# Strassen's seven products in the last matrix product of a retention and bilinear feed-forward kernel

## The chip, the core and the metric

The kernel runs on one NeuronCore of a Trainium2 chip. The core has a matrix engine (TensorE, PE in the profile; its weight loads are listed apart as PEld), a vector engine (VectorE, DVE), a scalar engine (ScalarE, ACT), a general engine (GpSimd, POOL) and an engine that here only issues DMAs (SyncE, SP). Each has its own instruction queue and works through it in order; semaphores tie the queues together. TensorE reads SBUF and writes PSUM; VectorE and ScalarE carry results from PSUM to SBUF. The metric is the device time of one execution in microseconds, lower is better.

## The reference

```python
q, k, v = float32 [8, 8, 576, 64]                  # batch, head, position, head dim
scores = (q @ k.transpose(0, 1, 3, 2)) / sqrt(64)
gamma  = 1.0 - 2.0 ** (-5.0 - arange(8))           # one decay per head
D[h, i, j] = gamma[h] ** (i - j) if i >= j else 0
ret = (scores * D) @ v
x   = ret.transpose(0, 2, 1, 3).reshape(4608, 512) # tokens x (head, dim)
a, b = x @ w_a, x @ w_b                            # both [512, 1536]
out = ((a * b) @ w_out).astype(float32)            # w_out [1536, 512]
```

The first part is retention: attention with an exponential decay in place of a softmax. The second is a bilinear feed-forward layer over all 4608 tokens. The last product, with w_out, is the one that is changed.

## The kernel before

**Feed-forward blocks.** The 4608 tokens go through the feed-forward part in ten blocks: 512, 256, 256 and then seven of 512 tokens (`blocks`, L111). The seven start at token 1024. `ffn_block` (L850) is a generator that writes one block's instructions. For each of the twelve slices F of 128 of the 1536 inner columns it makes four products with w_a into a PSUM tile `pa` (L872), which ScalarE copies to `ha` in bf16 (L880), four products with w_b into `pb` (L887), and VectorE multiplies the two into the bf16 tile `hT` (L892), which holds the inner activations of the block as [128 inner rows, 12 slices, 512 tokens]. Then come the rows: for each 128 tokens, twelve products with `hT` as the stationary operand and w_out (`wo_sb`) as the moving one, 512 columns wide, into a tile `po` (L908). ScalarE and VectorE copy `po` to `osb` in turn (L917, L919), and SP stores it. The final 128 tokens are done in pieces of 256, 128 and 128 columns, each in a `po` tile of its own.

All of `pa`, `pb` and `po`, and the tiles `kv` below, come from one ring of four PSUM tiles of 512 float32 columns, one PSUM bank each (`ps_ffn`, tag "ab", L89). A product into a new tile waits until the last reader of the tile four places earlier has ended. `hT` has one buffer, `osb` eight.

**Retention.** The tokens are also cut into eighteen groups of 256, a "pair" of 128 each (`PAIRS`, L50). For group n, `load_pair` (L140) has SP load q, k and v into a ring of staging tiles (`stage`, four buffers each of qf, kf, vf). `ahead(n)` (L509) has POOL cast q and k to bf16 (L519, L523) and multiply v by its decays (L530). `turn(n)` (L536) has SP transpose q and k by DMA (L542) and, from n = 11 on, load group n+2. `stretch(into, outof)` (L756) writes the products: for the group `outof` the part of the output that comes from states (`open_outputs`, `from_states`, L670), for `into` the sums of keys by values (`keyed`, L573, into two tiles `kv` of the ring of four) and the scores (`matched`, L642, which needs the transposed q and k), and for `outof` the part from its own keys (`keys_into`, L683). The work of other engines that follows is put on a list `later`: four additions that read `kv` (VectorE, L600), two calls of `scaled` (VectorE writes the group's x, L696), a conversion with the first mask, a conversion with the second mask (ScalarE L603 to L611, VectorE L651). Every `pop()` in the feed-forward code writes the next item of that list into the queues; `flush()`, at each block's end and each stretch's start, writes all that are left. The last stretches and `outputs_alone` (L746) write their sums of two PSUM tiles in a constant tile `both` first (`summing`, L730).

**Order.** The program is written by hand order (`manual_schedule`). The main loop at the end walks through all blocks; each `yield` of `ffn_block` gives the cost of what was just written, in units of one 512-column product, and whether this is an edge. At an edge every entry of `todo` whose due time has come is called. A block of 512 tokens counts 96 units for w_a and w_b and 48 for the rows. In the rows there is an edge after every four products. Most `stretch` calls are due 116 and 44 units before the start of a block (`starts`), the casts 70 and the transposes 38 units before their stretch (L1084 to L1108); those of the early groups have fixed times, for example `stretch(8, 7)` at unit 408.

**Stores.** From the fourth block on `store` is called right after a copy. Rows of the first blocks wait in `held` and are stored at listed times, since SP and the DMA engines are then busy with loads.

## Time and profile before

| what | value |
|---|---|
| median of 3 runs | 324.75 us (324.59 to 324.81) |
| profiled execution: span, first to last instruction | 323.1 us |
| median less span (what lies around the profiled span) | 1.65 us |
| granted TensorE clock, mean | 0.999 of full speed |
| TensorE busy | 313.8 us, 97% |
| VectorE busy | 166.2 us, 51% |
| ScalarE busy | 130.7 us, 40% |
| POOL busy | 118.8 us, 37% |
| 512-column products of the rows (L908) | 379 ns each as recorded |
| weight loads | 98 ns each, beside the products |

The profile has one execution. A matmul's recorded duration holds its way through the pipeline, so two in a row overlap; the rate of TensorE is read from their starts. A line of the timeline gives start, duration, engine, line, operation, written tile <- read tiles, shapes and count, and in brackets how long the engine was idle before and what ended that. A line of groups gives count, busy us, mean ns of one, idle before and its releasers. A line of a window gives its length, then the busy us of PE, PEld, DVE, ACT and POOL, the granted clock, the busy share of the DMA engines and GB/s.

### The profile page before, as it was taken

To read this page: it belongs to the slowest core of one execution; us is meant where nothing else is said; L and a number is where in the kernel's file an instruction comes from. 1 tells how busy PE (TensorE), PEld (TensorE's weight loads), DVE (VectorE), ACT (ScalarE), POOL (GpSimd) and SP (SyncE) were. 2 spreads that over 40 slices of the span, in tenths; PEclk is the share of its full clock that TensorE was granted. 3 is DMA by queue.
4 is the path that set the end of the run, shared out by engine and by line. 5 is a ranking of instruction groups with operands and counts; after the bars stand their busy time and mean duration, and the time that the engine had idled before them with its cause. 6 is when DMAs were issued, how large, how long until landed. Compare 5 with 4: busy or idle time off the path is not lost.

```text
span 323.1 us, 8622 instructions
## 1 busy us (share of the span) xinstructions
PE 313.8 (97%) x3569; PEld 164.0 (51%) x3607; DVE 166.2 (51%) x296; ACT 130.7 (40%) x289; POOL 118.8 (37%) x159
## 2 busy tenths in 40 slices
PE   7899999999999999999999999999999999999996
PEld 3554457778444555454454545454545444444444
DVE  5745346667437654745374527561666256514311
ACT  7745653436435533523253324342433243313321
POOL 4990077564744355447264305450520000000000
PEclk9999999999999999999999999999999999999999
DMA  8999999999899989999999168935940510031013
GB/s 215 253 201 206 260 228 180 192 181 206 180 189 227 199 199 204 287 208 232 230 220 215 70 143 191 212 79 145 210 72 26 137 37 2 2 97 32 1 25 107
DMA packets 146487, 50.90 MB, mean 158 GB/s; under 512 B 126736, under 2 KB 141968, under 8 KB 146448
## 3 DMA queue, kind: packets, MB, share of 16 engines
q1 hardware_dynamic: 140112, 45.37, 66.3%
q0 software_dynamic: 5808, 4.72, 9.3%
q8 instruction: 28, 0.46, 0.6%
q10 hardware_dynamic: 528, 0.26, 0.3%
q14 instruction: 11, 0.09, 0.1%
HBM read 37.75 MB, written 9.44 MB: 146 GB/s over the span
## 4 chain that ended last, share of the span: by engine, by line
PE 93%; DMA 2%; POOL 1%; issue 1%; SPq 1%; DVE 0%; POOLq 0%
PE pb L887 29%; PE pa L872 28%; PE po L908 27%; DMA vf<-in_v_dram 2%; PE po L834 2%; PE o L683 1%; PE sc L642 1%; PE o L670 1%; PE kv L573 1%; SPq L159 1%; POOL vb L326 1%; PE pa L823 1%; PE o L465 0%; PE tp L334 0%; POOL wb_sb L266 0%
## 5 line engine op out<-in xcount | busy, mean ns | idle before, releaser
L892 DVE TENSOR_TENSOR hT<-ha,pb 128x512 bf16<-128x512 bf16 (+1 forms) x120 | 75.8, 632 | 91.4 <-PE pb L887 83.3
L887 PE MATMUL pb<-xT,wb_sb 128*128 128x512 bf16 (+1 forms) x473 | 111.3, 357 | 0.5
L880 ACT CAST ha<-pa 128x512 bf16<-128x512 f32 (+1 forms) x120 | 64.8, 542 | 112.8 <-PE pa L872 108.3
L872 PE MATMUL pa<-xT,wa_sb 128*128 128x512 bf16 (+1 forms) x457 | 108.0, 357 | 1.1 <-issue 0.6
L908 PE MATMUL po<-wo_sb,hT 128*128 128x512 bf16 (+2 forms) x419 | 89.6, 367 | 1.6 <-issue 1.4
L887 PEld LDWEIGHTS <-wb_sb 128*128 128x128 bf16 x480 | 46.9, 98 | 46.3
L872 PEld LDWEIGHTS <-wa_sb 128*128 128x128 bf16 x472 | 45.4, 98 | 44.8 <-DVE sums L600 0.2
L908 PEld LDWEIGHTS <-hT 128*128 128x128 bf16 x432 | 40.4, 98 | 44.4
L519 POOL CAST qkb<-qf 64x1024 bf16<-64x1024 f32 x15 | 15.4, 1030 | 65.4 <-DMA qf<-in_q_dram 64.4
L530 POOL TENSOR_TENSOR vb<-vf,vs 128x1024 bf16<-128x1024 f32 (+1 forms) x17 | 28.8, 1699 | 13.0 <-DMA vf<-in_v_dram 4.9
L919 DVE COPY osb<-po 128x512 f32<-128x512 f32 (+2 forms) x16 | 10.4, 649 | 38.8 <-PE po L908 38.8
L917 ACT COPY osb<-po 128x512 f32<-128x512 f32 (+1 forms) x20 | 11.4, 572 | 46.3 <-PE po L908 43.4
L519 POOL CAST qkb<-kf 64x1024 bf16<-64x1024 f32 (+1 forms) x17 | 15.9, 933 | 16.7 <-DMA kf<-in_k_dram 16.3
L600 DVE TENSOR_TENSOR sums<-kv,sums 128x256 f32<-128x256 f32 x44 | 18.6, 423 | 2.8 <-PE kv L573 0.8
L651 DVE TENSOR_TENSOR sT<-sc,mask 128x512 bf16<-128x512 f32 x30 | 19.5, 680 | 0.0
L523 POOL CAST qkb<-kf 64x512 bf16<-64x512 f32 (+1 forms) x34 | 18.6, 574 | 1.0
L523 POOL CAST qkb<-qf 64x512 bf16<-64x512 f32 x30 | 17.6, 614 | 0.6
L696 DVE TENSOR_TENSOR xT<-o,qs 128x512 bf16<-128x512 f32 x24 | 15.4, 680 | 2.6 <-PE o L683 2.6
L603 ACT CAST states<-sums 64x512 bf16<-64x512 f32 x26 | 16.0, 617 | 0.3
L316 POOL CAST qkb<-kf 128x512 bf16<-128x512 f32 x4 | 2.5, 612 | 15.9 <-DMA kf<-in_k_dram 15.9
L360 DVE TENSOR_TENSOR sT<-sc,mask_s 128x1024 bf16<-128x1024 f32 x6 | 7.3, 1222 | 1.5 <-PE sc L352 1.3
L935 PE MATMUL w<-ones 128*128 128x512 bf16 x17 | 6.5, 497 | 1.5 <-DVE idxp_f L204 1.5
(96 smaller groups left out, 173.5 us busy)
## 6 DMA issues: line engine op xcount, KB each, us to landing
qf<-in_q_dram SPq DMA_DIRECT2D x32, 256.0 KB, 4.7
vf<-in_v_dram SPq DMA_DIRECT2D x32, 256.0 KB, 5.0
kf<-in_k_dram SPq DMA_DIRECT2D x31, 256.0 KB, 5.1
out_dram<-osb SPq DMA_DIRECT2D x25, 256.0 KB, 3.2
out_dram<-osb SPq DMA_DIRECT2D x21, 128.0 KB, 2.7
wo_sb<-in_moe_w_out_dram POOLq DMA_DIRECT2D x3, 512.0 KB, 15.9
qf<-in_q_dram SPq DMA_DIRECT2D x8, 128.0 KB, 3.6
kf<-in_k_dram SPq DMA_DIRECT2D x8, 128.0 KB, 3.6
```

What stands on the lines that cost most here:

```text
L519: nc.gpsimd.tensor_copy(qkb[0:64, w, e], t[0:64, e])
L523: nc.gpsimd.tensor_copy(to[:, :, 1 - r], fro[:, :, r])
L530: nc.gpsimd.tensor_tensor(vb[:, e].rearrange("p (h d) -> p h d", d=D), t[:, e].rearrange("p (h d) -> p h d", d=D), decay[:, at], op=ALU.mult)
L600: nc.vector.tensor_tensor(sums[:, i], own, prev, op=ALU.add)
L603: return [lambda r=r: nc.scalar.copy(to(half(1 - r)), fro(half(r))) for r in (0, 1)]
L651: nc.vector.tensor_tensor(sT[:, on].rearrange("p c k s -> p (c k) s"), sc[:, on].rearrange("p c k s -> p (c k) s"), mask3.unsqueeze(1).to_ ...
L696: nc.vector.tensor_tensor(x_of(t0, 128).rearrange("p c (a s) -> p c a s", a=2), o[:, :, :, kp].rearrange("p a c s -> p c a s"), qs[:, :, s ...
L872: nc.tensor.matmul(pa[:, 0:n], wa_sb[:, c, fs], xT[:, c], start=(c == 0), stop=(c == NC - 1))
L880: nc.scalar.copy(ha[:, 0:n], pa[:, 0:n])
L887: nc.tensor.matmul(pb[:, 0:n], wb_sb[:, c, fs], xT[:, c], start=(c == 0), stop=(c == NC - 1))
L892: nc.vector.tensor_tensor(hT[:, F, 0:n], has[F][:, 0:n], pb[:, 0:n], op=ALU.mult)
L908: nc.tensor.matmul(po[:, 0:width], hT[:, F, u * 128:(u + 1) * 128], wo_sb[:, F, cols], start=(F == 0), stop=(F == NF - 1))
```

## The change

From token 1024 on (group 4, `MIXED`) the product with w_out is done by Strassen's scheme. A group of 256 tokens is the left matrix, with even and odd tokens as its two row halves and the inner slices F even and odd as its two contraction halves; w_out's column halves of 256 are the right one's. With a11, a12, a21, a22 (row half, contraction half) and b11 to b22, seven half-size products are made, each of six matmuls of 256 columns, 42 a group in place of 24 of 512 columns.

What comes with it:

- `scaled` writes x so that even and odd tokens of a group lie apart, as two operations of 256 columns in place of one of 512.
- `weight_sums`: ten VectorE operations of 768 bf16 elements make b11+b22, b11+b12, b21+b22 and, in place, b12-b22 and b21-b11, at times 150 to 180 and 290 to 314 of the list.
- `row_sums`: per block ten VectorE operations on `hT`, all operands bf16 in SBUF, five of 1024 elements from F = 7 on (two after each F) and five of 512 after F = 11, before the edge of F = 11. Two of each five are in place.
- `rows_mixed`: the products and their combination. Products 3 and 4 go to the halves of one tile (m34), product 1 to a tile m1, products 5 and 2 to the halves of a tile m52; products 7 and 6 are later added to the halves of m34. ScalarE copies m34 and m1 to SBUF, VectorE combines.
- It offers an edge only at the end of a group, and `total` counts 21/24 for the rows, so that a changed block has 138 units.
- A group is stored by one DMA of 512 KB (four of 128 KB for the two groups made of batch ends, three pieces for the last).
- `stage` goes from four buffers to three, `osb` from eight tiles to four of double size, `both` moves into the ring of vf, and some early constants give up their space to the new tiles when the first changed block begins.

```diff
@@ pools @@
+    MIXED = 4
-    stage = pool("stage", 4)
+    stage = pool("stage", 3)
-    o_pool = pool("osb", 8)
+    o_pool = pool("osb", 4)
...
+    wo_sums = big.tile([128, 3, NF // 2, DM // 2], BF16)
@@ scaled @@
+            if n >= MIXED:
+                at = s0 + kp * step
+                x = x_of(place(n) * 256, 256).rearrange(
+                    "p c (k q a s) -> p q c a k s", k=2, q=2, a=2)[:, kp]
...
+                for a in (0, 1):
+                    nc.vector.tensor_tensor(x[:, :, a], of[:, a], by[:, :, a],
+                                            op=ALU.mult)
+                return
@@ summing @@
-    both = const.tile([128, 2, 2, HP, 64], FP32)
+        both = stage.tile([128, 2, 2, HP, 64], FP32, tag="vf", name="both")
@@ new functions @@
+    def weight_sums(step):
...
+        out, one, other, op = [(to[0], b11, b22, ALU.add),
+                               (to[1], b11, b12, ALU.add),
+                               (to[2], b21, b22, ALU.add),
+                               (b12, b12, b22, ALU.subtract),
+                               (b21, b21, b11, ALU.subtract)][step // 2]
+        nc.vector.tensor_tensor(out, one, other, op=op)
+
+    def row_sums(hT, sums, p0, p1):
+        even, odd = (hT[:, 2 * p0:2 * p1].rearrange(
+            "p (f e) (g k s) -> p e k f g s", e=2, g=2, k=2)[:, e]
+            for e in (0, 1))
+        a11, a21, a12, a22 = even[:, 0], even[:, 1], odd[:, 0], odd[:, 1]
+        to = [sums[:, i, p0:p1] for i in range(3)]
+        return [lambda e=e: nc.vector.tensor_tensor(*e[:3], op=e[3])
+                for e in ((to[0], a11, a22, ALU.add),
+                          (to[2], a12, a22, ALU.subtract),
+                          (a12, a11, a12, ALU.add),
+                          (to[1], a21, a11, ALU.subtract),
+                          (a21, a21, a22, ALU.add))]
+
+    def rows_mixed(G, hT, sums, g):
+        t0 = 256 * g
+        def product(to, way, ps, begins):
+            for p in ps:
+                even, odd = 2 * p, 2 * p + 1
+                rows, cols = {
+                    1: (sums[:, 0, p, g], wo_sums[:, 0, p]),
+                    2: (hT[:, even, t0 + 128:t0 + 256], wo_sb[:, even, 0:WIDE]),
+                    3: (hT[:, even, t0:t0 + 128], wo_sb[:, even, WIDE:]),
+                    4: (hT[:, odd, t0 + 128:t0 + 256], wo_sb[:, odd, 0:WIDE]),
+                    5: (hT[:, odd, t0:t0 + 128], wo_sb[:, odd, WIDE:]),
+                    6: (sums[:, 1, p, g], wo_sums[:, 1, p]),
+                    7: (sums[:, 2, p, g], wo_sums[:, 2, p])}[way]
+                nc.tensor.matmul(to, rows, cols, start=(begins and p == 0),
+                                 stop=True, skip_group_check=True)
+                yield 0.5, False
...
+        own, lo, hi = bank("m34")
+        for part in (range(NP2 - 1), (NP2 - 1,)):
+            yield from product(lo, 3, part, True)
+            yield from product(hi, 4, part, False)
+        straight = late["parts"].tile([128, 512], FP32, tag="m34", name="straight")
+        nc.scalar.copy(straight, own)
+        pop()
+        first, one, _ = bank("m1")
+        yield from product(one, 1, range(NP2), True)
+        ones_ = late["parts"].tile([128, WIDE], FP32, tag="m1", name="m1s")
+        nc.scalar.copy(ones_, one)
+        pop()
+        cross, five, two = bank("m52")
+        yield from product(five, 5, range(NP2), True)
+        pop()
+        yield from product(two, 2, range(NP2), False)
+        less = late["parts"].tile([128, 2, WIDE], FP32, tag="m52", name="less")
+        nc.vector.tensor_tensor(
+            less, ones_.unsqueeze(1).to_broadcast([128, 2, WIDE]),
+            cross.rearrange("p (k m) -> p k m", k=2), op=ALU.subtract)
+        flat = osb.rearrange("p k m -> p (k m)")
+        nc.vector.tensor_tensor(flat[:, WIDE:3 * WIDE], cross, straight,
+                                op=ALU.add)
...
+        pop()
+        for way, to, at, i in ((7, hi, slice(0, WIDE), 0),
+                               (6, lo, slice(3 * WIDE, 4 * WIDE), 1)):
+            yield from product(to, way, range(NP2), False)
+            nc.vector.tensor_tensor(flat[:, at], to, less[:, i], op=ALU.add)
...
+            pop()
+        if not last:
+            store_mixed(G, osb)
+        yield 0, True
@@ ffn_block, after the multiplication into hT and its pop() @@
+                if tok0 >= 256 * MIXED:
+                    if F == 7:
+                        chores += row_sums(hT, sums, 0, 4)
+                    elif F == NF - 1:
+                        chores += row_sums(hT, sums, 4, 6)
+                    for _ in range(2 if F < NF - 1 else len(chores)):
+                        if chores:
+                            chores.pop(0)()
...
+        if tok0 >= 256 * MIXED:
+            for g in range(n // 256):
+                yield from rows_mixed(tok0 // 256 + g, hT, sums, g)
+            return
@@ planner @@
-    def total(n):
-        return NF * 2 * NC * n / 512 + NF * n / 128
+    def total(n, mixed):
+        return NF * 2 * NC * n / 512 + (21 / 24 if mixed else 1) * NF * n / 128
...
+    todo += [(150 + 6 * step, weight_sums, (step,)) for step in range(6)]
+    todo += [(290 + 8 * step, weight_sums, (6 + step,)) for step in range(4)]
```

More of the change, by code (lines that the diff above doesn't have):

```diff
@@ L86, with pools_mixed @@
     ha_pool = pool("ha", 6)
-    o_pool = pool("osb", 8)
+    o_pool = pool("osb", 4)
+    late, early = {}, ExitStack()
+    begin = early.enter_context(tc.tile_pool(name="begin", bufs=1))
+    ctx.push(early)
+    def pools_mixed():
+        if not late:
+            early.close()
+            for name in ("hsum", "parts"):
+                late[name] = early.enter_context(
+                    tc.tile_pool(name=name, bufs=1))
     PS = bass.MemoryType.PSUM
@@ L180 @@
     make_identity(nc, identity)
-    mask_s = const.tile([128, 2, 2, 64], BF16)
+    mask_s = begin.tile([128, 2, 2, 64], BF16)
     nc.gpsimd.memset(mask_s, 1.0)
@@ L199, in make_masks @@
                 pattern=[[1, 64]], channel_multiplier=-1)
-    ones = const.tile([128, 512], BF16)
+    ones = begin.tile([128, 512], BF16)
     nc.vector.memset(ones, 1.0)
@@ L214 @@
                              bias=0.0, scale=-math.log(gammas[h]))
-    qs_o = const.tile([128, HP, 256], FP32)
+    qs_o = begin.tile([128, HP, 256], FP32)
     qs = const.tile([128, HP, S + 64], FP32)
@@ L250, in pair_tables @@
             make_qs(qs, (step - 5) // 2, s0, s0 + part)
-    state_after = const.tile([128, 2, HP, 128], BF16)
+    state_after = begin.tile([128, 2, HP, 128], BF16)
     own_sums = [const.tile([128, HP, 64], FP32, name=f"own{n}")
@@ L694, in scaled @@
         def scaled(kp):
+            if n >= MIXED:
+                at = s0 + kp * step
+                x = x_of(place(n) * 256, 256).rearrange(
+                    "p c (k q a s) -> p q c a k s", k=2, q=2, a=2)[:, kp]
+                by = qs[:, :, at:at + 128].rearrange(
+                    "p c (a s k) -> p c a k s", a=2, k=2)
+                of = o[:, :, :, kp].rearrange(
+                    "p a c (s k) -> p a c k s", k=2)
+                for a in (0, 1):
+                    nc.vector.tensor_tensor(x[:, :, a], of[:, a], by[:, :, a],
+                                            op=ALU.mult)
+                return
             t0 = place(n) * 256 + kp * 128
@@ L841, in rows_together @@
                     continue
-                osb = o_pool.tile([128, DM], FP32, tag="osb", name="osb")
+                osb = half_of(o_pool, u, [DM], FP32, "osb")
                 if u % 2 == 0:
@@ L848, in rows_together @@
                 yield 1, True
+    WIDE = DM // 2
+    def weight_sums(step):
+        p0 = 3 * (step % 2)
+        even, odd = (wo_sb[:, 2 * p0:2 * p0 + 6].rearrange(
+            "p (f e) m -> p e f m", e=2)[:, e] for e in (0, 1))
+        b11, b12 = even[:, :, 0:WIDE], even[:, :, WIDE:]
+        b21, b22 = odd[:, :, 0:WIDE], odd[:, :, WIDE:]
+        to = [wo_sums[:, i, p0:p0 + 3] for i in range(3)]
+        out, one, other, op = [(to[0], b11, b22, ALU.add),
[4 more added lines that the diff above has]
+        nc.vector.tensor_tensor(out, one, other, op=op)
@@ new lines, in store_mixed @@
+    def store_mixed(G, osb, cols=slice(0, 2 * DM)):
+        n = place(G)
+        for kp, r0, m, b, s0 in rows_of(n):
+            if n in LEFT:
+                p0 = kp * 64 + r0 // 2
+                m //= 2
+            elif kp == 1:
+                continue
+            else:
+                p0, m = 0, 128
+            rows = out[b * S + s0:b * S + s0 + 2 * m].rearrange(
+                "(p two) c -> p (two c)", two=2)
+            nc.sync.dma_start(rows[:, cols],
+                              osb[p0:p0 + m].rearrange("p k c -> p (k c)")
+                              [:, cols])
@@ new lines, in rows_mixed, with bank @@
+    def rows_mixed(G, hT, sums, g):
[14 more added lines that the diff above has]
+                yield 0.5, False
+        def bank(name):
+            t = ps_ffn.tile([128, 512], FP32, tag="ab", name=name)
+            return t, t[:, 0:WIDE], t[:, WIDE:]
+        NP2 = NF // 2
+        last = G == NP - 1
+        osb = o_pool.tile([128, 2, DM], FP32, tag="osb", name="osb2")
+        own, lo, hi = bank("m34")
[21 more added lines that the diff above has]
+                                op=ALU.add)
+        if last:
+            store_mixed(G, osb, slice(WIDE, 3 * WIDE))
+        pop()
[3 more added lines that the diff above has]
+            nc.vector.tensor_tensor(flat[:, at], to, less[:, i], op=ALU.add)
+            if last:
+                store_mixed(G, osb, at)
+            pop()
+        if not last:
+            store_mixed(G, osb)
+        yield 0, True
@@ L853, in ffn_block @@
         hT = h_pool.tile([128, NF, 512], BF16, tag="h", name="hT")
+        chores = []
+        if tok0 >= 256 * MIXED:
+            pools_mixed()
+            sums = late["hsum"].tile([128, 3, NF // 2, 2, 128], BF16, tag="hsum",
+                                  name="hsum")
         f0 = 0
@@ L898, in ffn_block @@
             yield from rows_together(tok0, hT, (0, 1))
+        if tok0 >= 256 * MIXED:
+            for g in range(n // 256):
+                yield from rows_mixed(tok0 // 256 + g, hT, sums, g)
+            return
         for u in range(2 if tb == 0 else 0, n // 128):
-            final = tok0 + (u + 1) * 128 == NTOK
-            osb = o_pool.tile([128, DM], FP32, tag="osb", name="osb")
-            edges = (0, DM // 2, 3 * DM // 4, DM) if final else (0, DM)
-            for part in range(len(edges) - 1):
-                cols = slice(edges[part], edges[part + 1])
-                po = ps_ffn.tile([128, 512], FP32, tag="ab", name="po")
-                width = cols.stop - cols.start
-                for F in range(NF):
-                    nc.tensor.matmul(po[:, 0:width],
-                                     hT[:, F, u * 128:(u + 1) * 128],
-                                     wo_sb[:, F, cols],
-                                     start=(F == 0), stop=(F == NF - 1))
-                    if F in (2, 5, 8):
-                        pop()
-                    if F < NF - 1:
-                        yield width / 512, F % 4 == 3
-                if n == 256 or (u + part) % 2 == 0:
-                    nc.scalar.copy(osb[:, cols], po[:, 0:width])
-                else:
-                    nc.vector.tensor_copy(osb[:, cols], po[:, 0:width])
-                if tb < 3:
-                    held.append((tok0 // 128 + u, cols, osb))
-                else:
-                    store(tok0 // 128 + u, cols, osb)
-                pop()
-                yield width / 512, True
+            osb = half_of(o_pool, u, [DM], FP32, "osb")
+            po = ps_ffn.tile([128, 512], FP32, tag="ab", name="po")
+            for F in range(NF):
+                nc.tensor.matmul(po, hT[:, F, u * 128:(u + 1) * 128],
+                                 wo_sb[:, F],
+                                 start=(F == 0), stop=(F == NF - 1))
+                if F in (2, 5, 8):
+                    pop()
+                if F < NF - 1:
+                    yield 1, F % 4 == 3
+            if n == 256 or u % 2 == 0:
+                nc.scalar.copy(osb, po)
+            else:
+                nc.vector.tensor_copy(osb, po)
+            held.append((tok0 // 128 + u, slice(0, DM), osb))
+            pop()
+            yield 1, True
     gate = const.tile([1, 64], BF16)
@@ L1029 @@
             starts[i] = at
+        at += total(n, tok >= 256 * MIXED)
         tok += n
-        at += total(n)
     def early_casts():
```

## The prediction

> **What bounds the kernel now.** I read the page's busy line and chain first, then the timeline for TensorE's step, then a window per block, then VectorE's groups by shape.

> ```profile
> span 323.1 us, 8622 instructions
> PE 313.8 (97%) x3569; PEld 164.0 (51%) x3607; DVE 166.2 (51%) x296; ACT 130.7 (40%) x289; POOL 118.8 (37%) x159
> ...
> PE 93%; DMA 2%; POOL 1%; issue 1%; SPq 1%; DVE 0%; POOLq 0%
> ```

> TensorE is the bound. Everything else is hidden behind it, so the question is what a product costs and whether TensorE is still fed.

> ```profile
> 50.29 0.60 PE L872 MATMUL pa<-xT,wa_sb 128*128 128x256 bf16 x4
> 50.73 0.60 PE L887 MATMUL pb<-xT,wb_sb 128*128 128x256 bf16 x4
> ...
> 294.96 1.03 PE L887 MATMUL pb<-xT,wb_sb 128*128 128x512 bf16 x4
> 295.16 0.59 ACT L880 CAST ha<-pa 128x512 bf16<-128x512 f32 x1 [1.14 <-PE pa L872]
> 295.61 0.74 PEld L872 LDWEIGHTS <-wa_sb 128*128 128x128 bf16 x4
> 295.82 1.03 PE L872 MATMUL pa<-xT,wa_sb 128*128 128x512 bf16 x4
> 296.09 0.69 DVE L892 TENSOR_TENSOR hT<-ha,pb 128x512 bf16<-128x512 bf16 x1 [1.04 <-PE pb L887]
> ```

> Read starts, not durations. Four 256-column products step 0.437 us (50.29 to 55.97, 52 products: 109.2 ns each), each with its own weight load; four of 512 columns step 0.864 (215.9 ns each). A reader on VectorE starts 0.27 after the next group of products has started (296.09 against 295.82); TensorE, where it waits for another engine, starts 0.05 after that one's end.

> ```profile
> 155.20:188.60 33.40, 32.98 (x388) 16.11 (x390) 17.29 (x30) 12.71 (x25) 13.31 (x15) 1.00 0.82 166
> ```

> The window of one block (busy us of PE, PEld, DVE, ACT, POOL, then the granted clock): TensorE idles 0.4 us of 33.4, VectorE half the time. What fails next is VectorE's order, not its total.

> ```profile
> L651 DVE TENSOR_TENSOR sT<-sc,mask 128x512 bf16<-128x512 f32 x30 | 19.5, 680 | 0.0
> L600 DVE TENSOR_TENSOR sums<-kv,sums 128x256 f32<-128x256 f32 x44 | 18.6, 423 | 2.8 <-PE kv L573 0.8
> ...
> L919 DVE COPY osb<-po 128x512 f32<-128x512 f32 x14 | 9.7, 691 | 34.7 <-PE po L908 34.7
> ...
> L338 DVE COPY qkT<-tp 128x512 bf16<-128x512 bf16 x6 | 2.5, 423 | 2.5 <-ACT qkT L338 1.2 <-PE tp L334 1.2
> ```

> A VectorE operation takes 0.42 us for 256 float32 columns, 0.69 for 512, and the next starts 0.09 before its end (two L651 take 1.28); all-bf16 runs at twice the rate.

> **Part 1, seven products.** A group of 256 tokens took 24 products of 215.9 ns, 5.18 us; it takes 42 of 109.2, 4.59. Fourteen groups: -8.3 us. The weight loads grow with the products but stay covered, as in the 109.2 row.

> **Part 2, the last two products of a group.** Products 3 and 4 share one PSUM bank (m34) by halves; 7 and 6 are added to it later. The order written is: product 7, VectorE reads its half, product 6 into the other half, VectorE reads that. If a bank's accesses are kept in the written order, product 6 waits for the read. From the group's start: 3 and 4 end at 1.31, 1 at 1.97, 5 at 2.62, 2 at 3.28, 7 at 3.93. VectorE: `less` 3.55 to 4.24, the middle sum 4.15 to 4.84, product 7's sum (256 columns) 4.75 to 5.17. Product 6 starts at 5.22 in place of 3.93 and ends at 5.88. Wait 1.29 a group, +18.1 us for fourteen. Nothing is queued on TensorE that could pass it; the next group and the next block stand behind it. The old kernel has no such pattern (it gives even the final 128-column piece a tile of its own, L905), so no row shows it: the bounds are 0, if halves are independent, and 1.29. I take 1.29: every old reader starts after all products into its bank (DVE hT at 296.09 behind the whole `pb`), which is what order by bank would look like, and nothing speaks for the other.
> [...]

> **Part 3, VectorE's new work.** Per block ten row sums (five of 1024, five of 512 bf16 elements, both inputs in SBUF), and per group two 512-column and two 256-column operations in place of one copy. Row sums: at L338's rate 0.69 and 0.42, 5.6 us a block; at the float32 rate 1.22 and 0.69, 9.6. I take the first, the nearest row in type. In a clean block (the last) they cost nothing: the five small ones end 2.6 us after F=11, when TensorE wants the last at 3.1. [...]
> Six of the seven blocks are not clean, because of the planner. A block now counts 96+42=138 units, and a group offers an edge only at its end. So `stretch` due at the next start -44 falls at unit 94: right after F=11 (before: four products into the rows). Its two kv banks come next in the ring of four, and product 5's bank is then kv's. VectorE goes: hT, five row sums (to +0.99 us after the stretch's end), four additions of kv (0.46 apart; the third frees the bank at 2.33), two scalings, `less`. Product 5 starts at 2.39, not 1.97; `less` at 4.15, not 3.97; a mask (0.68) stands between the middle sum and product 7's. The group ends at 7.07 instead of 5.88: +1.2, four blocks, +4.8. In the first of the changed blocks (tokens 1024 to 1535) a stretch falls behind F=10: one of its scalings stands before the row sums, so product 1 waits 0.3, and the rest with both masks stands before `less`: the first group ends at 7.37, +1.5. In the block with `outputs_alone` (tokens 3584 to 4095) two `summed` stand there: 7.78, +1.9. Together +8.2.
> `stretch(8, 7)` is fixed at unit 408; edges are at 405 and 426, so it comes at the very end of its block, whose successor needs its x. From that end: kv's bank is free at 0.75, kv read from 1.32, additions to about 3.2, four half scalings to 4.5. TensorE has 1.55 of stretch in that time: +3.0.

> ```profile
> L426 DVE TENSOR_TENSOR own<-own,second x1: 565/565/565, 49.9 to 49.9; 128x256 f32<-128x256 f32 x1
> ...
> L696 DVE TENSOR_TENSOR xT<-both,qs x6: 691/691/1358, 231.7 to 282.0; 128x512 bf16<-128x512 f32 x6
> ```

> VectorE operations with both inputs in SBUF were longer exactly where POOL ran casts (565 against 423, 1358 against 691). They lost 0.14 and 0.67, 0.4 in the mean; with ten row sums a block and POOL 46% busy in the windows of the four blocks from 86.2 to 222.2 that is 7.4 us of VectorE, between none and all of it on the path. I take a third, as the big sums lie under F=7 to 10, where TensorE has work: +2.5. Ten weight sums of 768 elements (0.56 each): six lie in the half block of tokens 512 to 767, where `hT` may be 0.62 late before TensorE lacks a bank. I take +0.5, the ends are 0 and, with POOL against each, 4.

> **Part 4, queues.**

> ```profile
> out_dram<-osb SPq DMA_DIRECT2D x25, 256.0 KB, 3.2
> ...
> qkT<-qkb SPq DMA_TRANSPOSE x30, 3.6
> ```

> `turn` due at unit 122 now follows the group's end, so on SP it stands behind a store that waits for the last sum: store at +0.75 after the block, transposes at 1.2 and 2.6, landing some 3.2 later at 5.8; with 512 KB instead of 256 ahead of them up to 6.7. `matched` wants them 24 units and 0.6 us into the next block, at 5.8 (before: 32 units in, and the transposes issued at 187.1, 1.5 before the block's end). So 0 to 0.9; I take 0.3 for four blocks: +1.2. `stage` from four to three buffers: each load issues after the cast three pairs before it has ended (pair 10's first at 116.1, pair 7's last cast 97.1; the nearest is pair 6, 73.7 against 53.8): nothing, nor do `both` in that ring (its neighbours were cast a block before) or four double output tiles. ACT gains 0.37 a group with 60% idle. The tail: last product to end was 0.27+0.29+2.5; now 0.42 for 256 columns and a 128 KB store (1.9 against 1.5): +0.5.

> **Sum.** -8.3 +18.1 +8.2 +3.0 +2.5 +0.5 +1.2 +0.5 = +25.7. The profiled span 323.1 becomes 348.8; the median stands 1.65 above the span, so 350.5 us.

> **Rivals.**
> A. Row sums at the float32 rate. VectorE then falls more than a bank behind at F=9 (2.9 us of work in 1.73), and the last five take 3.1 us instead of 1.8: 1.6 to 2.9 us in each of seven blocks, 16.6, and 1 for the weight sums: 368 us. For: no row has two bf16 inputs in SBUF; against: L338.
> B. Halves of a bank are independent, VectorE's order binds: without the 1.29 the stretch blocks keep 1.5 each (product 5's bank, next group's bank), the first 1.2, the `outputs_alone` one 1.6: -8.3+8.8+3.0+3.2 = +6.7, 331.5.
> C. The other side: halves independent, and VectorE keeps ahead, so only the late stretch and tail remain: -8.3+3.5+0.5, 320.5, faster. It decides at a wait of 0.59 a group (5.18-4.59); the wait for product 7's read alone, with VectorE free, would be 0.27+0.42+0.05=0.74, so any ordering of the bank excludes it.
> D. The halves save nothing, each held up by its own weight load (98 ns busy), so the 8.3 stays out: 358.8. The 109.2 step of blocks with a load for each product speaks against it.

> **Chances.** Forecast 0.75, A 0.11, B 0.07, C 0.05, D 0.02. The forecast's own range is 336 (no stretch or POOL cost on the path) to 362 (all of it, weight sums at worst). The range 335 to 368 leaves out B, C and half of A, under 2 in 10. Within 0.2% (0.65 us, what three runs can tell): 0.01; faster 0.05; slower 0.94.

> **What would show it.** Seven products: groups of 42 with 0.109 steps. Part 2: in each group an idle of TensorE before six products, about 1.3 us, ended by VectorE's sum. Part 3: row sums of 0.69 and 0.42; idle before product 5 ended by L600; an idle of some 3 us between tokens 1535 and 1536. Part 4: `matched` waiting for a DMA. I am wrong if TensorE goes from product 7 to 6 without a gap.

## The result, and the profile after

| what | before | after |
|---|---|---|
| median | 324.78 us (324.59 to 324.96) | 371.1 us (370.57 to 376.42, 4 runs) |
| ratio, 95% interval | 1 | 1.1414 [1.1386, 1.1442] |
| profiled span | 323.1 us | 368.9 us |
| TensorE idle in the span, idle times above 0.15 us summed | 4.9 us | 43.3 us |
| granted TensorE clock, mean | 0.999 | 0.967 |

The change costs 46.3 us. The median takes in one slow execution of 376.42 us; the other three lie at 370.6 to 371.6, so the differences from 371.1 given below can be up to 0.5 us too large. The direction was forecast and the size was not: 25.7 was the sum, and 371.1 lies above the range's end of 368.

The page of the changed kernel, its busy line, its row of the granted clock in 40 slices and its chain:

```profile
span 368.9 us, 9213 instructions
PE 320.5 (87%) x3804; PEld 191.3 (52%) x3835; DVE 240.7 (65%) x445; ACT 135.9 (37%) x302; POOL 124.2 (34%) x159
...
PEclk9999999999999899989999999968999999989999
...
PE 61%; DVE 21%; issue 6%; DMA 6%; SPq 3%; POOL 1%; ACT 1%; DVEq 0%; ACTq 0%; POOLq 0%
```

TensorE was 93% of the chain and is 61%; VectorE went from nothing to 21%. No engine is full: 87% and 65%. This is a kernel that waits. The clock row now has slices at 8 and 6.

The waits of TensorE in the changed kernel (engine, line, releaser: us in total, times, longest):

```profile
PE m L938 <- DVE osb L978: 19.4, 14, 3.0
PE m L938 <- DVE sums L614: 10.6, 4, 4.1
PE sc L656 <- DMA qkT<-qkb: 3.6, 4, 1.7
PE pa L1013 <- DVE xT L718: 2.7, 1, 2.7
PE kv L587 <- DVE hT L1033: 2.1, 2, 1.7
```

In order: product 6 for VectorE's read of product 7, once in each of the fourteen groups; product 5 for a bank that the additions of `kv` hold; the scores for their transposes; a block's first product for x, once; `kv` for a bank. All but the last were steps of the forecast. A step from one product to the next is longer than the listed idle by some 0.15 us, since the idle is counted from a modelled end; below, a wait is the step less that of a product that doesn't wait.

A group in the last block, which no stretch disturbs (timeline, lines of other engines left out):

```profile
353.36 1.47 PE L938 MATMUL m<-wo_sb,hT 128*128 128x256 bf16 x12
...
356.66 0.82 PE L938 MATMUL m<-wo_sums,hsum 128*128 128x256 bf16 x6
356.93 0.69 DVE L966 TENSOR_TENSOR less<-m1s,m 128x512 f32<-128x512 f32 x1 [0.56 <-PE m L938]
357.53 0.68 DVE L970 TENSOR_TENSOR osb<-m,straight 128x512 f32<-128x512 f32 x1
358.13 0.41 DVE L978 TENSOR_TENSOR osb<-m,less 128x256 f32<-128x256 f32 x1
358.60 0.82 PE L938 MATMUL m<-wo_sums,hsum 128*128 128x256 bf16 x6 [1.13 <-DVE osb L978]
359.25 0.60 PE L938 MATMUL m<-wo_sb,hT 128*128 128x256 bf16 x4
```

From 353.36 to 359.25 are 5.89 us; the forecast said 5.88. Six products take 0.65 (358.60 to 359.25), so product 7 ended at 357.31; product 6 then waited 1.28 until `less`, the middle sum and product 7's own sum were through. Parts 1 and 2 came out as worked.

VectorE's row sums and POOL's work ahead of product 5 in the slowest group of the changed kernel (12.55 us; the timelines of the two engines):

```profile
238.39 0.83 DVE L899 TENSOR_TENSOR hsum<-hT 128x512 bf16<-128x512 bf16 x1
239.25 0.72 DVE L899 TENSOR_TENSOR hT<-hT 128x512 bf16<-128x512 bf16 x1
239.90 2.12 DVE L899 TENSOR_TENSOR hsum<-hT 128x512 bf16<-128x512 bf16 x1
242.05 0.42 DVE L899 TENSOR_TENSOR hT<-hT 128x512 bf16<-128x512 bf16 x1
```

```profile
238.25 1.45 POOL L537 CAST qkb<-kf 64x512 bf16<-64x512 f32 x2
239.78 1.96 POOL L544 TENSOR_TENSOR vb<-vf,vs 128x1024 bf16<-128x1024 f32 x1
```

An operation of this kind took 0.42 us alone (a mean of 421 ns in the run without casts, below) and took 2.12 here beside POOL's multiplication: it ended at 242.02, 0.28 us after that one (241.74).

Windows of 3.41 us around two of the waits (length, busy us of PE, PEld, DVE, ACT, POOL, then the granted clock):

```profile
156.90:160.31 3.41, 0.93 (x10) 0.59 (x8) 3.20 (x8) 1.23 (x4) 0.48 (x1) 1.00 0.00 0
160.31:163.72 3.41, 3.12 (x16) 1.99 (x14) 2.71 (x7) 1.60 (x3) 0.00 (x0) 0.50 0.02 5
...
238.83:242.24 3.41, 0.97 (x9) 0.62 (x7) 3.34 (x4) 0.96 (x2) 2.82 (x3) 1.00 0.00 0
242.23:245.64 3.41, 1.78 (x9) 1.29 (x10) 3.18 (x9) 1.73 (x4) 0.00 (x0) 0.50 0.00 0
245.64:249.06 3.42, 2.32 (x12) 1.49 (x11) 2.36 (x5) 0.31 (x1) 0.00 (x0) 0.50 0.01 2
```

TensorE idles 2.5 us of the first window, and in the whole next window the clock is half. In the half-rate windows a 256-column product steps 213 ns in place of 110. There are seven such windows, 23.9 us in all; the steps in them, less those of the same products at the full clock, add up to 8.9 us. Before had none as long as it had products.

### The profile page after: what moved, and what is told of

It reads as the page before. It is cut to its first block, busy times and chain, and to the rows that moved or that the text cites. A ratio compares the mean times of both kernels' runs of the same rounds, so it can differ in the third digit from the quotient of the medians.

```text
span 368.9 us, 9213 instructions
## 1 busy us (share of the span) xinstructions
PE 320.5 (87%) x3804; PEld 191.3 (52%) x3835; DVE 240.7 (65%) x445; ACT 135.9 (37%) x302; POOL 124.2 (34%) x159
## 4 chain that ended last, share of the span: by engine, by line
PE 61%; DVE 21%; issue 6%; DMA 6%; SPq 3%; POOL 1%; ACT 1%; DVEq 0%; ACTq 0%; POOLq 0%
PE pa L1013 19%; PE pb L1028 18%; PE m L938 14%; DVE hsum L899 5%; DMA qkT<-qkb 4%; PE po L1056 4%; DVE hT L899 3%; DVE hT L1033 3%; DVE less L966 2%; DVE osb L978 2%; DVE sums L614 2%; SPq L556 2%; DMA vf<-in_v_dram 1%; DVE xT L718 1%; PE po L859 1%
## 5 line engine op out<-in xcount | busy, mean ns | idle before, releaser
L1013 PEld LDWEIGHTS <-wa_sb 128*128 128x128 bf16 x472 | 45.3, 98 | 46.3 <-DVE xT L718 2.8
L938 PE MATMUL m<-wo_sb,hT 128*128 128x256 bf16 x336 | 47.5, 297 | 10.6 <-DVE sums L614 10.6
L938 PE MATMUL m<-wo_sums,hsum 128*128 128x256 bf16 x252 | 38.4, 293 | 19.6 <-DVE osb L978 19.4
L938 PEld LDWEIGHTS <-hT 128*128 128x128 bf16 x336 | 34.8, 106 | 19.4 <-DVE sums L614 11.7
L938 PEld LDWEIGHTS <-hsum 128*128 128x128 bf16 x252 | 26.2, 104 | 27.0 <-issue 22.1
L899 DVE TENSOR_TENSOR hsum<-hT 128x1024 bf16<-128x1024 bf16 (+1 forms) x42 | 32.6, 804 | 0.4
L954 ACT COPY straight<-m 128x512 f32<-128x512 f32 x14 | 8.2, 585 | 52.6 <-PE m L938 52.6
L966 DVE TENSOR_TENSOR less<-m1s,m 128x512 f32<-128x512 f32 x14 | 9.6, 686 | 26.2 <-PE m L938 26.2
L537 POOL CAST qkb<-kf 64x512 bf16<-64x512 f32 (+1 forms) x34 | 20.5, 630 | 1.0
L899 DVE TENSOR_TENSOR hT<-hT 128x1024 bf16<-128x1024 bf16 (+1 forms) x28 | 20.3, 725 | 0.5
L614 DVE TENSOR_TENSOR sums<-kv,sums 128x256 f32<-128x256 f32 x44 | 18.6, 423 | 2.0
L978 DVE TENSOR_TENSOR osb<-m,less 128x256 f32<-128x256 f32 x28 | 11.8, 420 | 12.2 <-PE m L938 12.2
## 6 DMA issues: line engine op xcount, KB each, us to landing
qf<-in_q_dram SPq DMA_DIRECT2D x32, 256.0 KB, 4.4
vf<-in_v_dram SPq DMA_DIRECT2D x32, 256.0 KB, 5.1
kf<-in_k_dram SPq DMA_DIRECT2D x31, 256.0 KB, 4.9
```

The lines of the kernel that those rows point to most:

```text
L537: nc.gpsimd.tensor_copy(to[:, :, 1 - r], fro[:, :, r])
L614: nc.vector.tensor_tensor(sums[:, i], own, prev, op=ALU.add)
L899: return [lambda e=e: nc.vector.tensor_tensor(*e[:3], op=e[3]) for e in ((to[0], a11, a22, ALU.add), (to[2], a12, a22, ALU.subtract), (a12 ...
L938: nc.tensor.matmul(to, rows, cols, start=(begins and p == 0), stop=True, skip_group_check=True)
L978: nc.vector.tensor_tensor(flat[:, at], to, less[:, i], op=ALU.add)
L1013: nc.tensor.matmul(pa[:, 0:n], wa_sb[:, c, fs], xT[:, c], start=(c == 0), stop=(c == NC - 1))
```

## The experiments

All changes are against the changed kernel unless said otherwise. "One run" stands for a single execution beside the kernel before. Changed kernels that were run several times have executions 2 to 6 us apart, so where a single run gains 2 or 3 us, the trace shows what changed and the time alone does not.

### Products 7 and 6 in a row

```diff
-        for way, to, at, i in ((7, hi, ...), (6, lo, ...)):
-            yield from product(to, way, range(NP2), False)
+        yield from product(hi, 7, range(NP2), False)
+        yield from product(lo, 6, range(NP2), False)
+        for to, at, i in ((hi, ...), (lo, ...)):
             nc.vector.tensor_tensor(flat[:, at], to, less[:, i], op=ALU.add)
```

> The changed kernel, with products 7 and 6 written one after the other and both VectorE sums behind them. The sums, the products and their number are the same. If the idle time before product 6 (19.4 us in 14 waits on VectorE's sum L978) is the order kept within one PSUM bank, it goes, and with it two of the stretches of half clock (those after the waits of 2.6 and 3.3 us): 344 to 349 us from 371.1. If the wait is VectorE being late in any case, it moves to the next group's product 1, which takes the same bank in the ring, and the time stays within 5 us of 371.

Measured: 350.5 us (349.4 to 352.3), ratio 1.0789 [1.0743, 1.0834]; 20.6 us less, a little short of the expected gain (344 to 349). The waits of TensorE with this order:

```profile
PE m L938 <- DVE sums L614: 11.1, 4, 4.1
PE sc L656 <- DMA qkT<-qkb: 4.6, 4, 2.0
PE pa L1014 <- DVE xT L718: 2.7, 1, 2.7
```

The largest wait is gone and none of its size has come in its place (one for `hT`, 1.5 us, is new); clean groups take 4.59 us, 42 products of 109 ns. So the wait was the written order, product after read in one bank, and the seven products are worth what they were said to be. What two accesses to one bank would do without that order no run shows. The clock mean stays at 0.968, 8.5 us lost: six half-rate windows are left, behind other waits, where I had expected two stretches to go.

### Without POOL's casts

```diff
     def ahead(n):
+        if n >= 10:
+            natural[FIRST + n, "pair"] = natural[FIRST + 9, "pair"]
+            return
```

> The changed kernel without POOL's casts and decays from pair 10 on: the later pairs use the cast tiles of pair 9, so their output is not the reference's; loads, transposes and all other engines' work stay. If POOL makes the row sums long (2.0 us in place of 0.42), the four waits before product 5 on the kv additions (10.6 us) fall to about 1 us each, as in the block where POOL is idle, and the half clock behind them goes: 354 to 360 us. If the row sums are long for a reason of their own, or the waits come from the bank ring alone, the waits stay at 2.5 to 4 us and the time at 368 to 371.

Measured: 359.3 us (one run), 11.8 less. The waits of TensorE and the row sums of 512 elements:

```profile
PE m L940 <- DVE osb L980: 21.3, 14, 3.0
PE m L940 <- DVE sums L616: 3.6, 4, 0.9
```

```profile
L901 DVE TENSOR_TENSOR hsum<-hT 128x512 bf16<-128x512 bf16 x21 | 8.3, 421 | 0.2
```

The wait before product 5 falls from 10.6 to 3.6, the row sums from 594 to 421 ns, and the half-rate loss from 8.9 to 4.6. These two give 7.0 and 4.3 us, while the waits before product 6 rise by 1.9 (19.4 to 21.3); the span is 11.3 us shorter, so about 2 us of gain are in smaller pieces. With POOL silent each stretch group takes 7.59 us, so VectorE's order alone costs 1.7 a block and not the 1.2 of the forecast: 1.07 before product 5 and 0.65 before product 6. The 0.65 shows in one of these four groups of the changed kernel; in the other three product 5 is so late that VectorE has caught up by product 6.

### Products that fill the idle

```diff
+        def fill(count):       # 256 columns into the unused half of m1
+            for _ in range(count):
+                nc.tensor.matmul(spare, wo_sums[:, 0, 0, 0:128], wo_sums[:, 0, 0], ...)
+        if G in (6, 8, 10): fill(16)          # before product 5
...
+            if way == 6 and G in (4, 14): fill(16)   # before product 6
```

> The changed kernel with 80 extra products of 256 columns (16 at each of five places, 1.75 us at full clock) into an unused half of the bank m1, at the five places where TensorE idles longest (before product 6 of groups 4 and 14, before product 5 of groups 6, 8 and 10); their results are not used. If the halved clock (23.9 us in five stretches) comes from TensorE idling about 2.5 us in a stretch of 3.4, the clock stays full, the waits end when they did, and the added work makes the kernel faster by 8 to 11 us: 360 to 363. If the clock falls for another reason, the time stays at 371 or rises by up to 9 us.

Measured: 366.8 us (365.3 to 370.7), ratio 1.1294 [1.1206, 1.1382]: 4.4 less with 80 products more. The direction is that of the clock theory, the size is half. None of the five filled places is followed by a half-rate window any more; but three windows remain, at 110.7, 134.6 and 182.4, behind waits that were not filled, with a loss of 4.6 us. The windows lie at another phase here, 1.5 us past a multiple of 3.41 from the span's start, where those of the changed kernel lie 3.3 past one. There the wait of `kv` that begins at 107.7 us was shared between two windows, with 1.37 and 0.51 us of idle in them, and no half rate followed; in the phase of this run, where the longest wait of `kv` is 2.1 us in place of 1.7, 107.3 to 110.7 is a single window, and the half rate begins at its end.

### The late stretch one edge earlier

```diff
-             (372, stretch, (7, 6)), (408, stretch, (8, 7))]
+             (372, stretch, (7, 6)), (404, stretch, (8, 7))]
```

> The changed kernel with stretch(8, 7) due at 404 in place of 408, so that it is written after the first group of its block and not after the second. If the 2.7 us wait of the next block's first product on x is this due time, it goes: 368 to 369 us. If another wait takes its place (the kv banks behind product 6), the time stays at 371.

Measured: 368.9 us (one run), 2.2 less, as expected. The wait of 2.7 us for x is gone from the list. The wait before product 5 rose by 2.1 and the half-rate loss fell by 3.1 (8.9 to 5.8): a part of the gain is not the wait itself.

### The kernel before, made to idle

```diff
-                nc.vector.tensor_tensor(hT[:, F, 0:n], has[F][:, 0:n],
-                                        pb[:, 0:n], op=ALU.mult)
+                times = {3: 6, 4: 7, 5: 8, 6: 9, 7: 10, 8: 12, 9: 16}
+                for _ in range(times.get(tb, 1) if F == 5 else 1):
+                    nc.vector.tensor_tensor(hT[:, F, 0:n], has[F][:, 0:n],
+                                            pb[:, 0:n], op=ALU.mult)
```

> The kernel before, with no product changed; in each of the seven blocks of 512 tokens VectorE repeats the multiply that writes hT of slice 5, 6, 7, 8, 9, 10, 12 and 16 times in turn, so that TensorE runs out of banks once a block, for about 1.4, 2.0, 2.6, 3.2, 3.8, 5.0 and 7.4 us (0.27 + 0.69 + 0.60 for each repetition, less 2.6 us of products that have banks). If the clock halves by itself after a stretch of 3.41 us in which TensorE idles more than about 2.1 us, the granted clock shows half-rate stretches behind the longer of these idles and none behind the first, each costs 1.2 to 1.7 us more than the idle, and the time is 325 + 25 of idles + 6 to 12. Rival: the half-rate stretches belong to the new products (narrow ones, more weight loads) and not to the idles; then the clock stays at 1.00 and the time is 350.

Measured: 355.0 us (one run), clock 0.976; just under the expected 356 to 362. Windows of this kernel, columns as above:

```profile
210.98:214.39 3.41, 2.05 (x8) 0.77 (x8) 3.31 (x7) 0.63 (x2) 1.03 (x1) 1.00 1.25 229
214.39:217.80 3.41, 2.79 (x13) 1.30 (x14) 2.39 (x4) 1.10 (x2) 3.21 (x5) 1.00 0.82 144
...
248.52:251.94 3.42, 0.83 (x5) 0.31 (x4) 3.32 (x6) 0.00 (x0) 0.00 (x0) 1.00 0.00 0
251.94:255.35 3.41, 3.41 (x9) 1.09 (x8) 2.36 (x4) 0.58 (x1) 0.00 (x0) 0.50 0.00 0
...
327.03:330.44 3.41, 0.00 (x0) 0.00 (x0) 3.24 (x6) 0.00 (x0) 0.00 (x0) 1.00 0.00 0
330.44:333.85 3.41, 1.71 (x5) 0.61 (x5) 3.34 (x6) 0.00 (x0) 0.00 (x0) 0.50 0.00 0
```

The old products lose their clock in the same way (0.50 behind windows with 2.59 and 3.41 us of idle), so it belongs to the idle. The shorter idles came out smaller than I meant (the first of 1.4 us, the next three in pieces of about 0.9) and tripped nothing; the last three, 2.4 to 3.4 us within one window, halved the clock of one or two windows each. The span is 30.2 us longer: 22.9 of waits, 6.3 of slower products (1.6, 2.1 and 2.5) and 1.0 in smaller pieces. The rival, that the half rate belongs to the new products, falls.

### Transposes ahead of the store

```diff
-        casts[n], turns[n] = placed[n] - 70, placed[n] - 38
+        casts[n], turns[n] = placed[n] - 70, placed[n] - 45
```

> The changed kernel with one number changed: the transposes of groups 11 to 17 are due 45 units before their stretch in place of 38, so that those of 11, 13, 15 and 17 are written at the end of the block's first group of rows, ahead of the store of the second. If the wait of the scores for the transposed q and k (3.6 us in the changed kernel) comes from standing behind that store, it goes and the time falls by 3 to 5 us, less what the earlier loads of two groups on do to POOL's and VectorE's meetings. Rival: the wait comes from POOL's late casts; then it stays above 3 us.

Measured: 362.0 us (one run), 9.1 less; more than expected. The wait for the transposes (3.6) is gone from the list, and the loads that follow them come earlier too: the wait before product 5 falls to 8.4, that of `kv` to 0.9, the half-rate loss to 7.2. In steps 4.2 + 2.3 + 1.2 + 1.7, less 0.7 that the waits before product 6 grow by: 8.7, the difference of the spans. The rival (POOL's late casts) falls.

### The second stretch between the groups of rows

```diff
-                 (starts[n] - 44, stretch, (n + 2, n + 1))
+                 (starts[n] - 21, stretch, (n + 2, n + 1))
                  if n + 2 < NP else
-                 (starts[n] - 44, outputs_alone, (n + 1,))]
+                 (starts[n] - 21, outputs_alone, (n + 1,))]
```

> The changed kernel with the second stretch of each block due 21 units before the next block in place of 44, so that it falls between the block's two groups of rows and no longer right behind F = 11 and the row sums. My theory of the wait before product 5 (10.6 us in the changed kernel): two parts, VectorE's order behind that stretch (1.2 us a block at least) and the row sums stretched by POOL. With the stretch elsewhere TensorE has 1.6 us less to do before product 5 but VectorE loses four additions there, so that wait falls to 3 to 6 us in all and the time by 4 to 8 us. Rival: the wait is POOL's alone; then it stays at 9 to 11 us and the time within 3 us of 371.

Measured: 358.6 us (one run), 12.5 less, beyond the expected 4 to 8. The waits of TensorE:

```profile
PE m L938 <- DVE osb L978: 21.3, 14, 3.1
PE sc L656 <- DMA qkT<-qkb: 3.6, 4, 1.7
...
PE m L938 <- DVE hT L899: 1.4, 3, 0.7
PE m L938 <- DVE hsum L899: 0.5, 1, 0.5
```

The 10.6 us before product 5 became 1.9, with POOL casting as before. Taking POOL away left 3.6, taking the stretch away leaves 1.9, and both together had made 10.6: a late row sum is short, but behind it stood the additions that free the bank. The waits before product 6 grow from 19.4 to 21.3, as without the casts. The half-rate loss falls from 8.9 to 3.2. The rival (POOL alone) falls.

### The four edits together

> The changed kernel with four edits together: products 7 and 6 in a row (the run before showed -20.6 us), transposes ahead of the store, second stretch between the groups of rows, and stretch(8, 7) due at 404. If the parts add: 371 - 20.6 - 4 - 2 - 6 - 3 for half-rate stretches that go with the idles = 332 to 338. It stays above the kernel before (325) as long as POOL's casts meet the row sums, which the run without casts put at 7.7 us of waits and 4.3 of clock. Rival: the parts are the same waits seen from different sides; then 343 to 349.

Measured: 327.8 us (325.6 to 332.0), ratio 1.0090 [1.0053, 1.0128]; better than my 332 to 338. Page and waits:

```profile
PE 308.6 (95%) x3804; PEld 185.9 (57%) x3835; DVE 231.2 (71%) x445; ACT 135.8 (42%) x302; POOL 124.1 (38%) x159
...
PEclk9999999999999999999999999999999999999999
```

```profile
PE m L938 <- DVE hT L899: 1.7, 3, 0.7
...
PE kv L587 <- DVE hT L1034: 1.1, 1, 1.1
PE pa L1014 <- DVE xT L718: 0.9, 1, 0.9
```

The single gains, 20.6 + 9.1 + 12.5 + 2.2 = 44.4, add up to 326.7. In this profiled execution (326.38 us) the longest wait is 1.5 us and the granted clock 1.000, without a half-rate window: the whole 8.9 us came back, where I had counted on 3. Not every execution is free of it: the four with a mean clock of 0.986 to 0.995 took 328.7 to 332.0 us, the five with 0.997 or more 325.6 to 327.8. With that 43.3 of the 46.3 us are given back; some 11 us of waits and small losses still take more than the 8.3 that the products save.

### What is left: row sums in three parts, outputs_alone, loads

```diff
-                    if F == 7:
-                        chores += row_sums(hT, sums, 0, 4)
-                    elif F == NF - 1:
-                        chores += row_sums(hT, sums, 4, 6)
+                    if F in (5, 9, NF - 1):
+                        chores += row_sums(hT, sums,
+                                           *{5: (0, 3), 9: (3, 5)}.get(F, (5, 6)))
```

> The four edits together, and the row sums cut in three parts by slices in place of two: slices 0 to 5 from F = 5 on, 6 to 9 from F = 9 on, and only the last pair of slices after F = 11, where five operations of 256 elements (some 0.25 us each uncontended) stand in place of five of 512. What is left of the wait in the first group of rows (excess over 4.59 us: 0.8, 2.0, 0.4 and 0.8 us in the first four blocks of the run with four edits) is VectorE's row sums behind F = 11 that meet POOL's casts. If so, it shrinks to 0.2 to 0.8 us a block, and the time falls by 2 to 3.5 us to 324 to 326. Rival: 35 more operations a kernel and POOL's meetings at other places take as much as they give; then it stays at 327 to 329.

Measured: 327.6 us, ratio 1.0064 [1.0040, 1.0088]; a miss. The first groups of the third and fourth block got shorter (5.00 and 5.40 to 4.68 and 5.04 us), those of the first two, where POOL casts most, longer (5.41 and 6.62 to 6.00 and 8.68).

```diff
-                 (starts[n] - 21, outputs_alone, (n + 1,))]
+                 (starts[n] - 90, outputs_alone, (n + 1,))]
-    todo += [(150 + 6 * step, weight_sums, (step,)) for step in range(6)]
+    todo += [(150 + 16 * step, weight_sums, (step,)) for step in range(6)]
```

> The same, and two shifts: outputs_alone due 90 units before the last block in place of 21 (it made the last block wait 0.9 us for its x and its own group 1.1 us), and the first six weight sums 16 units apart in place of 6 (they stand in half-size blocks, where a wait of 0.6 us for ScalarE appears that the kernel before does not have). If both waits go and none comes for them: 1 to 2 us less than the run without these two shifts. Rival: outputs_alone then stands before the row sums of its block, and product 1 or 5 waits there as long as before.

Measured: 326.5 us, ratio 1.0044 [1.0024, 1.0063], 1.1 less, as expected, though the two intervals overlap and the time alone does not settle it. In the profile the group behind outputs_alone takes 4.58 instead of 5.66, and the wait for ScalarE beside the weight sums is gone; the first two blocks still wait, 8.55 us in the second's first group.

```diff
-             (411.95, store_held, (2,)), (412.3, load_pair, (11, (K, V))),
-             (412.4, load_pair, (12,))]
+             (411.95, store_held, (2,)), (411.97, load_pair, (11, (K, V))),
+             (520, load_pair, (12,))]
```

> The run with the shifts of outputs_alone and weight sums, and two loads moved: k and v of group 11 ahead of group 10's transposes on SP, and group 12's three loads 96 units later, at the block's last but one edge. What POOL casts follows the loads: its casts of 11 and 12 fill 142.8 to 155.8 us of that run, where the second block's row sums and hT stand, and there the first group takes 8.55 us instead of 4.59. With group 11 cast before and group 12 after, that group falls to 5 to 6 us and the time by 2.5 to 3.5 us, to 323 to 324. Rival: the second block is late by VectorE's own work; then nothing changes there, and group 12's transposes, later, make its scores wait instead.

Measured: 325.0 us, ratio 1.0007 [0.9995, 1.0019]; 1.5 less (1.2 by the ratios, since the kernel before was 0.2 faster beside this run), not 2.5 to 3.5. The group of 8.55 takes 6.64, with one wait of 1.95 left in it, for hT.

### Seven products only from token 1536 on

```diff
-    MIXED = 4
+    MIXED = 6
...
-    todo += [(290 + 8 * step, weight_sums, (6 + step,)) for step in range(4)]
+    todo += [(434 + 8 * step, weight_sums, (6 + step,)) for step in range(4)]
```

> The same without the early due time of stretch(8, 7), and the seven products only from token 1536 on, so that the first of the seven blocks computes its rows by the eight half-size products, as the kernel before does (twelve 512-column products for each 128 tokens); its four weight sums move into the second block. The first block gained 1.2 us by seven products and lost 3.3 us to waits in the run before (0.35 before pb, 1.1 before the rows, 2.0 in the first group). If its two stretches and the weight sums on VectorE are why, 1.5 to 2.5 us less than the run beside it. Rival: the four weight sums bring the same waits to the second block; then within 1 us of it.

The run also has the load of group 12 due at 526 in place of 520, and the first block stores its rows right after each copy.

Measured: 322.4 us (320.9 to 324.0), ratio 0.9926 [0.9903, 0.9950]: faster than both kernels, 2.4 us (0.7%) below the kernel before and 48.7 below the change as made; 2.6 below the run beside it, where 1.5 to 2.5 was expected. Its page and waits:

```profile
span 320.2 us, 9183 instructions
PE 311.4 (97%) x3799; PEld 183.7 (57%) x3799; DVE 225.4 (70%) x455; ACT 135.1 (42%) x300; POOL 122.8 (38%) x159
```

```profile
PE m L938 <- DVE hT L1034: 1.4, 2, 0.8
PE o L684 <- DVE sT L665: 0.6, 1, 0.6
```

Twelve groups save 12 x 0.59 = 7.1 us by products; the span is 2.9 shorter than before. Most of the remaining 4.2 is in three groups that take 5.62, 4.86 and 5.80 us instead of 4.59 (2.5) and in a last product that stands 4.4 us before the end instead of 3.1. The third, fifth and seventh of the seven blocks, whose groups take 4.58 to 4.68 us, are 1.2 to 1.3 us shorter than before, the saving of two groups: the gain is that of the products and does not come from the due times alone.

The first block, with its old products, takes 34.70 us, as before (34.67); with seven products it had taken 36.98 and, in the run beside this one, 35.36. So there they had cost more in waits than their 1.2 us. But only 0.7 of the gain over the run beside it is in this block; the second block, which keeps its seven products, is 1.9 us shorter (35.95 to 34.01). Whether the moved due times or the shorter queue of VectorE in the first block did that, no run separates.

## Why the prediction was wrong, step by step

In spans of the one profiled execution, which is 45.8 us longer; waits from the steps of TensorE:

| step | forecast | measured |
|---|---|---|
| Part 1, seven products | -8.3 | -8.3 |
| Part 2, product 6 behind the read of product 7 | +18.1 | +17.9 (14 x 1.28) |
| Part 3, stretch, first and `outputs_alone` groups, VectorE's order | +8.2 | +8.7 (product 5: 4 x 1.07, the run without casts; product 6 beyond 1.28: 1.2, 0.65, 1.9; first group 0.6) |
| Part 3, POOL against row sums | +2.5 | +7.0 (wait before product 5 with and without casts) |
| Part 3, late stretch | +3.0 | +2.9 |
| `kv` behind a late `hT` | no term | +2.4 |
| Part 3, weight sums | +0.5 | +0.9 (the wait for ScalarE beside them) |
| Part 4, transposes | +1.2 | +4.2 |
| Part 4, tail | +0.5 | +0.8 |
| half clock | no term | +8.9 |
| sum | +25.7 | +45.4, of 45.8 |

**Right.** The price of the products, and with it rival D's end; the bank's order, to 0.01 us a group, which ends rivals B and C; the row sums at L338's rate, 0.68 and 0.42 us where POOL is silent, which ends rival A; the late stretch; the weight sums and the tail in size. (Rival B's sum takes 3.2 for terms that the forecast puts at 4.7 together; the gap before product 6 ends B either way.) That the time lies near rival A's 368 is chance: its mechanism is not there.

**Wrong, the largest: a term that is missing.** The forecast summed idles as if TensorE came back from each at the rate it had. The window shown of before had a granted clock of 1.00 beside 0.4 us of idle, and nothing asked what it would be beside 2.5. The steps themselves put waits of 2 to 3 us into the sum (the late stretch, the stretch groups), so the question was there. With this term alone left out of the measured 371.1 us, some 362 would remain, inside the range. The half-rate windows are 3.41 us long, at a granted clock of 0.50; the windows ahead of them were not idle all through, as the last section shows (0.93 and 0.97 us of products in the two shown above).

**Wrong in size: POOL.** The step "They lost 0.14 and 0.67, 0.4 in the mean ... I take a third" averaged over short meetings and then took the big sums' cover for all. A meeting with POOL's multiplication cost up to 1.7 us in one piece (2.12 and twice 2.01 against 0.42), and in three blocks it fell on the five small sums behind F = 11, which nothing covers. The upper bound I had, 7.4, was the right end. Nor had the big sums cover everywhere: in the first changed block one took 2.38 us beside POOL's multiplication (0.68 alone), `hT` came late behind it, and `kv` waited 1.73 us for the bank that `hT`'s operation reads. The sum had no term for that.

**Wrong in size: VectorE's order.** I had the row sums end 0.99 us after the stretch; they end 1.66 after it (282.84 against 281.18 in the block where POOL is silent), so product 5 waits 1.07 and not 0.42. That the row still comes out near its forecast is luck: where POOL makes product 5 later, the part before product 6 does not show.

**Wrong in size: transposes.** "0 to 0.9; I take 0.3": behind a 512 KB store they land 3.4 to 5.5 us after their issue, where I took 3.2 (the row that I showed has 3.6 as their median), and the scores wait 0.5 to 1.8 us a block, 1.05 in the mean. The value was too low, and so was the bound.

The misses have one sign. For POOL and for the transposes I had two ends and took a low third, and POOL's waits stand where VectorE's order does, behind F = 11, where a late operation makes the next late.

## What to carry to other kernels

A change that saves products and adds work on another engine is worth its saving only where that work has cover, so ask of each new operation which product waits for it and what else is written in front of it; here moving one read and three due times gave back 43 of 46 us. When the sum contains waits of 2 us and more on TensorE, price the clock as well as the wait: here the half-rate windows cost 8.9 us beside the waits themselves. If a stage's waits cost more than the change saves there, leave that stage out: six of seven blocks made a faster kernel than seven.

## What the runs showed of the hardware that I had not expected

The second is the size of one meeting of VectorE and POOL: 0.42 us became 2.12, as VectorE's operation ended only 0.28 us after the whole of POOL's instruction (1.96 us); two more row sums that met such a multiplication (1.93 and 1.96 us) took 2.01 each.
